# Windowed attention feeding a token and channel mixer: products with v per pair of heads, q and k parts a slot ahead

## Chip, cores and metric

The kernel runs on one core of a Trainium2 chip. The metric is the device time of one launch in microseconds (us). The engines named below are TensorE (PE, with PEld for its weight loads), VectorE (DVE), ScalarE (ACT), GpSimd (POOL) and SyncE (SP), which issues the DMAs.

## What is computed

Eight batches of eight heads, 576 positions, head width 64. Attention runs within a causal window of 128 with a bias that falls with distance; its output is the input of a mixer with a cosine and sine turn, a token mix and a channel mix.

```python
def _attn_ref(q, k, v):
    scores = scale * np.matmul(q, k.transpose(0, 1, 3, 2))
    ...
    mask = (rel >= 0) & (rel < window)
    scores = np.where(mask, scores + bias[None], -1000000000.0)
    scores = scores - np.max(scores, axis=-1, keepdims=True)
    attn = np.exp(scores)
    attn = attn / (np.sum(attn, axis=-1, keepdims=True) + 1e-09)
    return np.matmul(attn, v)

def _moe_ref(x, w_theta, w_tok_r, w_tok_i, w_ch):
    theta = x @ w_theta
    zr, zi = x * np.cos(theta), x * np.sin(theta)
    y = np.einsum('ts,bsd->btd', w_tok_r, zr) + np.einsum('ts,bsd->btd', w_tok_i, zi)
    u = x + y
    return u + np.maximum(u @ w_ch, 0.0)
```

## The kernel before

**Tiling.** Two heads make a pair, four pairs a batch. A pair's scores fall into five tiles: tile 0 goes to a bank of the pool `ps_m`, tiles 1 and 2, and 3 and 4, to two-bank buffers of `ps_s`. PSUM has eight banks here: two buffers of `ps_s` (4), one bank of `ps_a` (`acc`), three of `ps_m`. Operands are split into a high and a low part, so that one product is three matmuls: `qh`, `kh`, `ql`, `kl` in `split_pair` (ACT L336 and L339, DVE L337, POOL L340), `vh`, `vl` in `split_values` (ACT L361, POOL L362, DVE L363).

**A pair's way.** `weigh` (DVE L428) adds the bias and takes the row's limit, ACT L431 takes the exponential into `front` (tiles 0 to 2) and `back` (tiles 3 and 4). `flip` makes two fp16 parts of each half (`hl`, ACT L445 and DVE L447), and a DMA on SP turns them (L449) into `pt`. A slot later `Head.values` (L467) makes the products of `pt` with `vh` and `vl`, 27 matmuls a head, in `acc`, and `Head.finish` (L480) clears it into `x_sb` with three DVE instructions: L484 (the sums), L486 (reciprocal), L487 (the scaled copy of 128 x 320). `acc` has one buffer, so the second head's products wait for the first head's L487.

**Stages.** `start` does the attention of batch 0 and unpacks the weights (up to 73 us). Then follow, for each batch b, a `turn` (transposes of `x_sb`, theta, sine and cosine, parts `z_hi` and `z_lo`) and four slots of `attend(b + 1)`. A slot holds the scores of the next pair, the products with v of the present one, and steps of two generators for batch b: `mix` (token mix, three matmuls a step) and `channels`. TensorE's order is the order of the code (L72 pins it): `STEPS` says how many steps stand at the slot's front, behind the scores (two entries, in a row) and behind the first head's products. The last pair of numbers of a slot thus cover the first head's `finish` and the second head's. Slots 1 and 3 also end a group of four heads: `measure` (DVE L260) has taken the largest |v|, `spread_first` and `spread_scales` make a scale from it, with a small matmul `mm<-fixed` that waits for DVE L272.

**Order on DVE, ACT, SP.** The other engines' order comes from a scheduler with priorities (`high_priority`) and `issue_after`. `prepare(p + 3)`, behind the first head's `finish`, makes the q and k parts for the pair of the next slot and then issues the loads of the following pair into `qr` and `kr`, which have one buffer each. `kl` on POOL waits for `ql` by hand (L342).

## Times and profile before

| | us |
|---|---|
| median of three runs | 697.14 (696.0 to 699.99) |
| the profiled execution, its own time | 699.51 |
| its span in the trace | 697.7 |
| busy: PE, DVE, ACT, POOL | 632.0, 543.5, 502.1, 147.2 |
| mean granted TensorE clock | 0.978 of full speed |

Busy time is read per engine over the span. A row of waits names the engine, the buffer and line that waited, the engine and line waited for, and then the sum in us, the number of waits and the longest. A row of a timeline has start, duration, engine, line, operation and, in brackets, the idle time just before and what ended it.

### The profile page before, as it was taken

What the parts mean: (1) busy time and instruction counts of PE and PEld (TensorE: products, weight loads), DVE (VectorE), ACT (ScalarE), POOL (GpSimd) and SP (SyncE); (2) the same over time, 40 slices, a digit from 0 to 9 for tenths busy, and PEclk for the clock granted to TensorE, in tenths of its full rate; (3) what the DMA queues carried; (4) which work ended last, traced back from release to release, by engine and by line L of the source; (5) the groups of instructions that cost most, each with busy time, mean ns of one, the idle gap of its engine ahead of it and who ended that gap; (6) DMA issues with size and microseconds to landing.
All of it is one profiled execution on the core that took longest, in us unless ns stands there. A gap on an engine that the chain in (4) does not pass through costs nothing.

```text
span 697.7 us, 15147 instructions
## 1 busy us (share of the span) xinstructions
PE 632.0 (91%) x5738; PEld 537.4 (77%) x5738; DVE 543.5 (78%) x1463; ACT 502.1 (72%) x947; POOL 147.2 (21%) x198
## 2 busy tenths in 40 slices
PE   4899697689999999799989999799989999799998
PEld 3888475468877888688867888688867888689887
DVE  4989679788699868898689868898689968865722
ACT  6999379666986769766977769766977679745810
POOL 3010000433113112131212212131212212220220
PEclk9999999799999999999999999999999999999999
DMA  9954702769128840788036940677047930731001
GB/s 273 322 169 134 129 0 58 188 120 199 37 53 193 163 116 18 145 157 190 25 79 159 185 95 18 157 156 187 18 82 155 157 85 18 150 76 36 27 18 52
DMA packets 153257, 80.22 MB, mean 115 GB/s; under 512 B 126304, under 2 KB 142688, under 8 KB 153184
## 3 DMA queue, kind: packets, MB, share of 16 engines
q1 hardware_dynamic: 153184, 79.25, 49.7%
q8 instruction: 45, 0.74, 0.4%
q14 instruction: 28, 0.23, 0.1%
HBM read 39.39 MB, written 9.44 MB: 70 GB/s over the span
## 4 chain that ended last, share of the span: by engine, by line
ACT 38%; DVE 28%; PE 21%; issue 7%; DMA 4%; POOL 1%; SPq 0%; DVEq 0%; ACTq 0%; POOLq 0%
PE mm L75 16%; ACT hl L445 6%; ACT back L431 6%; ACT front L431 5%; DVE hl L447 5%; ACT g L552 3%; ACT z_hi L500 2%; ACT g L551 2%; DVE vl L363 2%; PE acc L75 2%; DVE ql L337 2%; DVE x_sb L487 2%; DVE front L428 2%; DVE g L556 2%; ACT xtf L525 2%
## 5 line engine op out<-in xcount | busy, mean ns | idle before, releaser
L75 PE MATMUL mm<-wtk_hi,z_hi 128*128 128x288 f16 x576 | 168.7, 293 | 0.4 <-DVE f L548 0.4
L75 PE MATMUL mm<-wtk_lo,z_hi 128*128 128x288 f16 x576 | 168.3, 292 | 0.0
L75 PE MATMUL mm<-wtk_hi,z_lo 128*128 128x288 f16 x576 | 168.1, 292 | 0.1
L75 PEld LDWEIGHTS <-z_hi 128*128 128x128 f16 x1152 | 109.5, 101 | 31.8 <-issue 1.3
L431 ACT ACTIVATE front<-front,fixed 128x256 f32<-128x256 f32 (+2 forms) x160 | 61.1, 448 | 45.8 <-DVE fixed L428 45.8
L75 PE MATMUL acc<-vh,pt 128*128 128x65 f16 x1044 | 60.5, 198 | 28.6 <-DVE x_sb L487 25.4
L75 PEld LDWEIGHTS <-pt 128*128 128x128 f16 x1566 | 56.4, 101 | 36.3 <-DVE x_sb L487 22.3
L340 POOL TENSOR_TENSOR kl<-kr,kh 128x576 fp32r<-128x576 f32 x31 | 48.5, 1564 | 136.6 <-DVE ql L337 40.1
L75 PEld LDWEIGHTS <-z_lo 128*128 128x128 f16 x576 | 57.6, 100 | 16.3 <-DVE z_lo L501 0.6
L622 POOL TENSOR_TENSOR u_lo<-xtf,u_hi 128x288 fp32r<-128x288 f32 x64 | 52.3, 837 | 58.1 <-ACT u_hi L620 31.0
L75 PE MATMUL acc<-vl,pt 128*128 128x64 f16 x522 | 56.7, 197 | 0.0
L361 ACT ACTIVATE vh<-vb,fixed 128x320 f16<-128x320 f32 x58 | 32.4, 562 | 33.7 <-PE acc L75 29.7
L431 ACT ACTIVATE back<-back,fixed 128x256 f32<-128x256 f32 x128 | 56.6, 498 | 0.0
L620 ACT CAST u_hi<-xtf 128x288 fp32r<-128x288 f32 x64 | 27.1, 426 | 37.5 <-DVE xtf L618 36.8
L362 POOL MEMSET vh<- 128x5 f16 x58 | 6.9, 119 | 220.6 <-PE acc L75 180.0
L75 PE MATMUL mm<-wth_hi,x_hi 128*128 128x512 f32 x160 | 48.0, 423 | 0.7 <-DVE x_hi L518 0.7
L75 PE MATMUL mm<-u_hi,wch_hi 128*128 128x288 f32 x256 | 47.2, 306 | 0.0
L428 DVE CUSTOM_DVE_ANT_0 back<-ps,bands 128x256 f32<-128x256 f32 x128 | 46.5, 419 | 0.1
L618 DVE SCALAR_TENSOR_TENSOR xtf<-mm,fixed,xtf 128x288 f32<-128x288 f32 x64 | 32.3, 508 | 18.1 <-PE mm L75 17.9
L75 PE MATMUL mm<-wth_lo,x_hi 128*128 128x512 f32 x160 | 44.8, 402 | 0.0
L75 PE MATMUL ps<-kh,qh 64*128 64x256 f32 (+1 forms) x256 | 43.8, 341 | 0.8 <-DVE fixed L428 0.8
L75 PE MATMUL mm<-u_lo,wch_hi 128*128 128x288 f32 x256 | 44.4, 295 | 0.0
(161 smaller groups left out, 1585.4 us busy)
## 6 DMA issues: line engine op xcount, KB each, us to landing
vb<-in_vx_dram SPq DMA_DIRECT2D x16, 650.0 KB, 5.1
out_dram<-xtf SPq DMA_DIRECT2D x64, 144.0 KB, 1.8
kr<-in_kt_dram SPq DMA_DIRECT2D x31, 288.0 KB, 3.5
qr<-in_qt_dram SPq DMA_DIRECT2D x31, 144.0 KB, 3.4
qr<-in_qt_dram SPq DMA_DIRECT2D x31, 128.0 KB, 3.4
xtf<-in_wch_dram SPq DMA_DIRECT2D x4, 512.0 KB, 4.8
z_hi<-in_wtok_dram SPq DMA_DIRECT2D x2, 576.0 KB, 6.3
z_lo<-in_wtok_dram SPq DMA_DIRECT2D x2, 576.0 KB, 6.3
```

The source lines that it names most:

```text
L75: ins = nc.tensor.matmul(*args, **kw)
L337: low = nc.vector.scalar_tensor_tensor(out=ql, in0=qr, scalar=sc, in1=qh.bitcast(F32), op0=ALU.mult, op1=ALU.subtract)
L340: rest = nc.gpsimd.tensor_tensor(out=kl, in0=kr, in1=kh.bitcast(F32), op=ALU.subtract)
L361: nc.scalar.activation(vh[:, :, :64], v, AF.Copy, scale=vs)
L428: self.weighed = nc.vector.tensor_tensor_reduce(out=sb, in0=ps, in1=bias, scale=2.0 ** -(2 * self.p % H + 1), scalar=3.0e38, op0=ALU.add, ...
L431: self.exps.append(nc.scalar.activation(sb, sb, AF.Exp, bias=least, scale=-1.0))
L445: self.copied = nc.scalar.activation(hl[:, 0], src, AF.Copy, scale=2.0 ** PEXP)
L447: self.lowered = nc.vector.scalar_tensor_tensor(out=hl[:, 1], in0=src, scalar=2.0 ** PEXP, in1=hl[:, 0], op0=ALU.mult, op1=ALU.subtract)
L552: nc.scalar.activation(g[:n], g[:n], AF.Sin, bias=halfpi[:n], scale=-RAD)
L618: nc.vector.scalar_tensor_tensor(out=xtf[:, m, cs], in0=y_ps[:, :HALF], scalar=st["back"], in1=xtf[:, m, cs], op0=ALU.mult, op1=ALU.add)
L620: nc.scalar.copy(u_hi[:, m, cs], xtf[:, m, cs])
L622: return nc.gpsimd.tensor_tensor(out=u_lo[:, m, cs], in0=xtf[:, m, cs], in1=u_hi[:, m, cs].bitcast(F32), op=ALU.subtract)
```

## The change

A pair's `values` now makes both heads' products, 54 matmuls in a row, in one two-bank buffer of `ps_s`; `ps_a` is gone and `ps_m` has four banks. `Pair.finish` clears both heads with three DVE instructions of twice the size. What stood between the two heads' products (the fourth entry of `STEPS`, `spread_scales`, a step of `channels`) now stands behind both. `split_pair` is cut into `split_high` (the two ACT instructions), called at the slot's front before the scores, and `split_low` (`ql`, `kl`), called with `prepare`'s loads behind the slot's last `weigh`; the parts made are those of the pair two slots on, one more than before. `vh` and `vl` have four buffers for two.

```diff
@@ -35,7 +35,7 @@
-RINGS = ([("mx", 2 * NT, 4)] + [("den", NT, 6)] + [("whole", 1, 3), ("vs", GROUP, 3), ("scale", GROUP, 4)]
+RINGS = ([("mx", 2 * NT, 4)] + [("den", 2 * NT, 3)] + [("whole", 1, 3), ("vs", GROUP, 3), ("scale", GROUP, 4)]
@@ -55,7 +55,7 @@
-    vp = ctx.enter_context(tc.tile_pool(name="vp", bufs=2))
+    vp = ctx.enter_context(tc.tile_pool(name="vp", bufs=4))
@@ -66,8 +66,7 @@
-    ps_a = ctx.enter_context(tc.tile_pool(name="ps_a", bufs=1, space=PSUM))
-    ps_m = ctx.enter_context(tc.tile_pool(name="ps_m", bufs=3, space=PSUM))
+    ps_m = ctx.enter_context(tc.tile_pool(name="ps_m", bufs=4, space=PSUM))
@@ -328,15 +327,23 @@
         batch_scale(0, scale[:, :8])
 
     def split_pair(p, raw):
+        return split_low(split_high(p, raw))
+
+    def split_high(p, raw):
 
         qr, kr = raw
         qh, ql = (qk.tile([128, S + 64], F32R, name=name) for name in ("qh", "ql"))
         kh, kl = (qk.tile([128, S], F32R, name=name) for name in ("kh", "kl"))
         sc = -0.125 * 2.0 ** (2 * p % H + 1)
         nc.scalar.activation(qh, qr, AF.Copy, scale=sc)
+        nc.scalar.copy(kh, kr)
+        return qr, kr, qh, ql, kh, kl, sc
+
+    def split_low(made):
+
+        qr, kr, qh, ql, kh, kl, sc = made
         low = nc.vector.scalar_tensor_tensor(out=ql, in0=qr, scalar=sc, in1=qh.bitcast(F32), op0=ALU.mult,
                                              op1=ALU.subtract)
-        nc.scalar.copy(kh, kr)
         rest = nc.gpsimd.tensor_tensor(out=kl, in0=kr, in1=kh.bitcast(F32), op=ALU.subtract)
         if pinned:
             after(rest, low)
@@ -351,10 +358,11 @@
             vb = group_v[n // GROUP]
             if n < 2 * PLAIN:
                 return (vb[:, k],), None, None
-            vs = first_scale[0][:, n:n + 1]
+            both = first_scale[0][:, n - n % 2:n - n % 2 + 2]
         else:
             vb, scale = group_v[n // GROUP]
-            vs = scale[:, k:k + 1]
+            both = scale[:, k - k % 2:k - k % 2 + 2]
+        vs = both[:, n % 2:n % 2 + 1]
         v = vb[:, k, :, :64]
         vh = vp.tile([128, 5, 65], F16, name="vh")
         vl = vp.tile([128, 5, 64], F16, name="vl")
...
@@ -454,38 +462,45 @@
                     at = 128 * n + (64 * to if i == 0 else 0)
                     self.pt[i, to, j] = [t[:, at:at + 128] for t in parts_of]
 
+        def values(self):
+            acc = ps_s.tile([128, 2, 512], F32, name="ps")
+            self.acc = acc[:, :, :NT * 65].rearrange("p e (i d) -> p e i d", d=65)
+            for head in self.heads:
+                e = head.h % 2
+                for i in (0, 2, 3, 4, 1) if e == 0 else (0, 1, 2, 3, 4):
+                    prods = []
+                    for j, c in enumerate(CHUNKS[i]):
+                        for a, part in enumerate(self.pt[i, e, j]):
+                            for o, v in enumerate(head.v):
+                                if a + o < len(head.v):
+                                    prods.append((part, v[:, c, :65 if o == 0 else 64]))
+                    for n, (l, r) in enumerate(prods):
+                        mm(self.acc[:, e, i, :r.shape[-1]], l, r, start=(n == 0), stop=(n == len(prods) - 1))
+
+        def finish(self, x_sb):
+            h = self.heads[0].h
+            den = rings["den"].take().rearrange("p (e i) -> p e i", e=2)
+            tiny = 1.0e-9 * (1.0 if self.early else 2.0 ** PEXP)
+            vs = self.heads[0].vs
+            if vs is None:
+                nc.vector.tensor_scalar(out=den, in0=self.acc[:, :, :, 64], scalar1=tiny, scalar2=None, op0=ALU.add)
+            else:
+                nc.vector.scalar_tensor_tensor(out=den, in0=self.acc[:, :, :, 64], scalar=tiny,
+                                               in1=vs[:, :, None].broadcast_to([128, 2, NT]), op0=ALU.add,
+                                               op1=ALU.mult)
+            nc.vector.reciprocal(out=den, in_=den)
+            x = x_sb[:, :, h * D:(h + 2) * D].rearrange("p i (e d) -> p e i d", e=2)
+            return nc.vector.tensor_tensor(out=x, in0=self.acc[:, :, :, :64],
+                                           in1=den[:, :, :, None].broadcast_to([128, 2, NT, D]), op=ALU.mult)
+
     class Head:
         def __init__(self, n, pair):
             self.n, self.pair = n, pair
             self.b, self.h = divmod(n, H)
-            self.tiny = 1.0e-9 * (1.0 if pair.early else 2.0 ** PEXP)
 
         def ready(self):
             self.v, self.vs, low = split_values(self.n)
             return low
-
-        def values(self):
-            self.acc = ps_a.tile([128, 512], F32, name="acc")
-            av = self.acc[:, :NT * 65].rearrange("p (i d) -> p i d", d=65)
-            for i in (0, 2, 3, 4, 1) if self.h % 2 == 0 else (0, 1, 2, 3, 4):
-                prods = []
-                for j, c in enumerate(CHUNKS[i]):
-                    for a, part in enumerate(self.pair.pt[i, self.h % 2, j]):
-                        for e, v in enumerate(self.v):
-                            if a + e < len(self.v):
-                                prods.append((part, v[:, c, :65 if e == 0 else 64]))
-                for n, (l, r) in enumerate(prods):
-                    mm(av[:, i, :r.shape[-1]], l, r, start=(n == 0), stop=(n == len(prods) - 1))
-
-        def finish(self, x_sb):
-            av = self.acc[:, :NT * 65].rearrange("p (i d) -> p i d", d=65)
-            den = rings["den"].take()[:, :, None]
-            scaled = {} if self.vs is None else {"op1": ALU.mult}
-            nc.vector.tensor_scalar(out=den, in0=av[:, :, 64:65], scalar1=self.tiny, scalar2=self.vs,
-                                    op0=ALU.add, **scaled)
-            nc.vector.reciprocal(out=den, in_=den)
-            return nc.vector.tensor_tensor(out=x_sb[:, :, self.h * D:(self.h + 1) * D], in0=av[:, :, :64],
-                                           in1=den.broadcast_to([128, NT, D]), op=ALU.mult)
 
 
     def turn(x_sb, st):
@@ -692,8 +706,14 @@
 
             steps = STEPS[min(g, 2)] if b > 1 else FIRST[g]
             step(mixing, steps[0])
+            ahead = p + DEPTH + 1
+            made = split_high(ahead, raw.pop(ahead)) if ahead < pairs else None
             for tiles in SCORES:
                 scores(tiles)
+            if made is not None:
+                with tc.issue_after(new.weighed.ins):
+                    parts[ahead] = split_low(made)
+                    prepare(ahead + 1)
             if new is not None:
                 new.flip(0)
                 new.flip(1)
@@ -706,9 +726,10 @@
             if scaled:
                 with tc.high_priority(FINISH):
                     spread_first(scaled)
-            one.values()
+            pair.values()
             with tc.high_priority(FINISH):
-                done = one.finish(x_sb)
+                done = pair.finish(x_sb)
+            step(mixing, steps[3])
             if scaled:
                 with tc.high_priority(FINISH):
                     spread_scales(scaled)
@@ -718,17 +739,11 @@
                         measure(*some)
                 if new is not None:
                     new.heads[0].ready()
-                with tc.issue_after(new.copied.ins) if new is not None else nullcontext():
-                    prepare(p + DEPTH + 2)
                 if b == 1 and g == 0:
                     with behind_all(new.exps):
                         step(late)
-            step(mixing, steps[3])
             if g >= 2 and (b > 1 or g == 3):
                 step(chans)
-            two.values()
-            with tc.high_priority(FINISH):
-                done = two.finish(x_sb)
             if new is not None:
                 with tc.issue_after(done.ins):
                     done = new.heads[1].ready()
@@ -768,18 +783,14 @@
                 pace(2 * len(tiles))
 
             if last is not None:
-                one, two = last.heads
                 last.flip(0)
                 scores(SCORES[0])
                 scores(SCORES[1])
                 last.flip(1)
-                one.values()
+                scores(SCORES[2])
+                last.values()
                 with tc.high_priority(FINISH):
-                    one.finish(x_sb)
-                scores(SCORES[2])
-                two.values()
-                with tc.high_priority(FINISH):
-                    two.finish(x_sb)
+                    last.finish(x_sb)
             else:
                 for tiles in SCORES:
                     scores(tiles)
```

The order of the built programs shows three places. First TensorE in slot 0 of a batch (matmuls and their weight loads), where the first head's products had ended and mixing matmuls lay ahead of the second head's. Before:

```order
2372 L75 MATMUL mm<-wtk_lo,z_hi 128x288
2373 L75 LDWEIGHTS z_lo
2374 L75 MATMUL mm<-wtk_hi,z_lo 128x288
2375 L75 LDWEIGHTS pt
2376 L75 MATMUL acc<-vh,pt 128x65
```

After, the seam between the two heads in the same slot (the first head's last product is row 2347):

```order
2345 L74 MATMUL ps<-vl,pt 128x64
2346 L74 LDWEIGHTS pt
2347 L74 MATMUL ps<-vh,pt 128x65
2348 L74 LDWEIGHTS pt
2349 L74 MATMUL ps<-vh,pt 128x65
```

The second head's products follow the first's at once, in another bank; the nine mixing matmuls that lay between now lie behind row 2401, ahead of the next slot's scores.

Second, DVE in slot 0 of the same batch, from the slot's `measure` to the first products of the next slot (`fixed` holds the small rings, `den` among them; `xtf` is the token mix's sum). Before:

```order
613 L260 TENSOR_REDUCE peak_107<-vb 128x2
614 L447 SCALAR_TENSOR_TENSOR hl<-front_105,hl 128x1024
615 L618 SCALAR_TENSOR_TENSOR xtf<-mm,fixed,xtf 128x288
616 L295 TENSOR_SCALAR peak_107<-peak_107 128x4
617 L618 SCALAR_TENSOR_TENSOR xtf<-mm,fixed,xtf 128x288
618 L447 SCALAR_TENSOR_TENSOR hl<-back,hl 128x1024
619 L484 TENSOR_SCALAR fixed<-acc,fixed 128x5
620 L486 RECIPROCAL fixed<-fixed 128x5
621 L487 TENSOR_TENSOR x_sb<-acc,fixed 128x5x64
622 L337 SCALAR_TENSOR_TENSOR ql<-qr,qh 128x640
623 L363 SCALAR_TENSOR_TENSOR vl<-vb,fixed,vh 128x320
624 L484 TENSOR_SCALAR fixed<-acc,fixed 128x5
```

After:

```order
571 L345 SCALAR_TENSOR_TENSOR ql<-qr,qh 128x640
572 L259 TENSOR_REDUCE peak_104<-vb 128x2
573 L455 SCALAR_TENSOR_TENSOR hl<-front_102,hl 128x1024
574 L633 SCALAR_TENSOR_TENSOR xtf<-mm,fixed,xtf 128x288 x2
575 L294 TENSOR_SCALAR peak_104<-peak_104 128x4
576 L455 SCALAR_TENSOR_TENSOR hl<-back,hl 128x1024
577 L488 SCALAR_TENSOR_TENSOR fixed<-ps,fixed 128x10
578 L491 RECIPROCAL fixed<-fixed 128x10
579 L493 TENSOR_TENSOR x_sb<-ps,fixed 128x2x5x64
580 L371 SCALAR_TENSOR_TENSOR vl<-vb,fixed,vh 128x320 x2
```

`ql`, and with it POOL's `kl`, has moved from behind the first clearing to ahead of both `hl` instructions; three clearing instructions stand where six did, in the place of the first head's.

Third, SP's queue in slot 0. Before, the slot's two turning DMAs, then the loads of q and k:

```order
100 L449 DMA_TRANSPOSE pt<-hl 128x16x128 x2
101 L238 DMA qr<-in_qt_dram 64x576
102 L239 DMA qr<-in_qt_dram 64x512
103 L240 DMA qr<-in_qt_dram 64x64
104 L241 DMA kr<-in_kt_dram 128x576
```

After:

```order
103 L237 DMA qr<-in_qt_dram 64x576
104 L238 DMA qr<-in_qt_dram 64x512
105 L239 DMA qr<-in_qt_dram 64x64
106 L240 DMA kr<-in_kt_dram 128x576
107 L457 DMA_TRANSPOSE pt<-hl 128x16x128 x2
```

The loads, which wait for the slot's `ql` and `kl` to have read `qr` and `kr`, now stand ahead of the turning DMAs.

## Rows read from the trace of the kernel before

**Rows 1.** The page's busy row, and its row of waits for `acc`.

```profile
PE 632.0 (91%) x5738; PEld 537.4 (77%) x5738; DVE 543.5 (78%) x1463; ACT 502.1 (72%) x947; POOL 147.2 (21%) x198
...
PE acc L75 <- DVE x_sb L487: 25.6, 16, 3.3
```

**Rows 2.** TensorE's waits from 190 to 612 us, six batches' slots.

```profile
PE acc L75 <- DVE x_sb L487: 20.1, 12, 3.3
PE ps L90 <- DVE x_sb L487: 2.3, 5, 0.5
PE mm L75 <- DVE fixed L272: 2.1, 5, 0.4
```

**Rows 3.** Timeline of slot 0 of one batch: DVE, then TensorE.

```profile
282.62 1.23 DVE L447 SCALAR_TENSOR_TENSOR hl<-back,hl 128x1024 f16<-128x1024 f32 x1 [0.54 <-ACT hl L445]
283.77 0.22 DVE L484 TENSOR_SCALAR fixed<-acc,fixed 128x5 f32<-128x5 f32 x1
284.02 0.19 DVE L486 RECIPROCAL fixed<-fixed 128x5 f32<-128x5 f32 x1
284.24 0.49 DVE L487 TENSOR_TENSOR x_sb<-acc,fixed 128x320 f32<-128x320 f32 x1
...
284.79 0.23 PE L75 MATMUL acc<-vh,pt 128*128 128x65 f16 x1 [3.29 <-DVE x_sb L487]
```

**Rows 4.** Windows of that batch's four slots (stretch, length, busy by engine, clock).

```profile
272.60:288.00 15.40, 12.11 (x141) 9.83 (x139) 13.57 (x39) 12.40 (x23) 1.77 (x3) 0.89 0.52 73
288.00:299.80 11.80, 11.01 (x139) 9.03 (x137) 10.66 (x37) 8.43 (x17) 3.35 (x5) 1.00 0.80 185
299.80:312.40 12.60, 12.31 (x150) 10.47 (x152) 11.80 (x41) 8.33 (x17) 3.73 (x8) 1.00 0.80 137
312.40:324.70 12.30, 11.89 (x143) 10.33 (x141) 11.23 (x35) 8.53 (x18) 2.87 (x5) 1.00 1.00 208
```

**Rows 5.** Windows of slot 0 of the four later batches.

```profile
350.20:365.80 15.60, 12.29 (x142) 9.89 (x139) 13.71 (x39) 12.53 (x23) 1.95 (x4) 0.90 0.40 81
428.20:443.40 15.20, 11.89 (x142) 9.49 (x140) 13.90 (x39) 12.54 (x23) 1.77 (x3) 0.93 0.40 79
506.20:520.90 14.70, 11.40 (x141) 9.19 (x140) 13.52 (x39) 12.54 (x23) 1.68 (x3) 0.96 0.38 75
584.20:598.40 14.20, 10.88 (x142) 9.01 (x139) 13.01 (x38) 12.53 (x23) 1.20 (x2) 1.00 0.35 70
```

**Rows 6.** Timeline of TensorE from a second head's products to the next scores.

```profile
596.52 0.20 PE L75 MATMUL acc<-vh,pt 128*128 128x65 f16 x1 [3.32 <-DVE x_sb L487]
...
600.06 0.28 PE L75 MATMUL ps<-kh,qh 64*128 64x256 f32 x2
```

**Rows 7.** POOL's `kl` beside DVE's `vl`, and two DVE groups (count | sum, mean ns).

```profile
322.03 1.44 POOL L340 TENSOR_TENSOR kl<-kr,kh 128x576 fp32r<-128x576 f32 x1 [3.50 <-DVE ql L337]
322.18 1.63 DVE L363 SCALAR_TENSOR_TENSOR vl<-vb,fixed,vh 128x320 f16<-128x320 f32 x1
...
L363 DVE SCALAR_TENSOR_TENSOR vl<-vb,fixed,vh 128x320 f16<-128x320 f32 x58 | 37.9, 657 | 0.5 <-ACT vh L361 0.5
L260 DVE TENSOR_REDUCE peak<-vb 128x2 f32<-128x640 f32 x26 | 21.1, 813 | 0.0
```

**Rows 8.** SP's queue and TensorE: turning DMAs of slot 0, products of slot 1.

```profile
281.23 4.70 SPq L449 DMA_TRANSPOSE pt<-hl  x2
...
pt<-hl SPq DMA_TRANSPOSE x58, 4.6
...
293.86 0.19 PE L75 MATMUL acc<-vh,pt 128*128 128x65 f16 x1
```

**Rows 9.** Batch 1's slots: one window, and TensorE's waits there.

```profile
103.50:174.00 70.50, 56.99 (x588) 45.96 (x589) 60.66 (x167) 49.29 (x97) 20.43 (x24) 0.88 0.64 138
...
PE mm L75 <- POOL kl L340: 3.9, 2, 2.5
PE acc L75 <- DVE x_sb L487: 3.3, 2, 2.7
```

More of the change, by code (lines that the diff above doesn't have):

```diff
@@ L364, in split_values @@
                                              op1=ALU.subtract)
-        return (vh, vl), vs, low
+        return (vh, vl), both, low
     TILES = [(512, 64, 384, 192, 0), (0, 128, 0, 128, 128), (128, 128, 0, 256, 0), (256, 128, 128, 256, 0),
@@ L673, in attend @@
             pair = first.pop(0)
-            one, two = pair.heads
             new = None
```

## The prediction

> **What bounds the kernel now.** I read the page's busy row first: TensorE is busy 632.0 us of the span [rows 1], so what it stands idle, some 66 us, is about all that a change of order can give, apart from time lost to a lower clock. The waits say where a good part of it goes: 25.6 us in 16 waits are for `acc`, the one bank that the second head's products find uncleared [rows 1]; 20.1 us in 12 of them lie between 190 and 612 us [rows 2]. The timeline shows one: TensorE has been idle 3.29 us when the second head's products start at 284.79, right behind the end of `x_sb` (284.24 + 0.49), and that clearing stood behind the `hl` of the back half, which had itself waited 0.54 us for ScalarE [rows 3]. So in slot 0 the nine mixing matmuls between the heads don't cover the clearing, which comes late on VectorE. The windows tell how much room there is behind it. Slot 0 takes 15.40 us with TensorE busy 12.11 at a granted clock of 0.89, VectorE 13.57; the other three slots run at clock 1.00 with TensorE busy 11.01, 12.31 and 11.89 of 11.80, 12.60 and 12.30 us, and VectorE 10.66, 11.80 and 11.23 [rows 4]. VectorE is thus never far behind TensorE, and in slot 0 it is ahead of it. That is what limits the change.
>
> **The waits for `acc`.** With both heads in two banks, the second head's products need no clearing, and the 20.1 us go. What takes their place is one ring further: a pair's two-bank buffer is the one that the next slot's scores of tiles 3 and 4 are written to, so they wait for `x_sb`. In slot 0, TensorE stood ready at 284.79 - 3.29 = 281.50. From the second head's first product to those scores is 600.06 - 596.52 = 3.54 us [rows 6], the same work in another order, so it now comes to them at 285.0. The clearing ended at 284.73; it comes later by the larger size and by what `kl` costs (both below: 0.3 and up to 0.7), so at up to 285.75. I take a new wait of 0.75 us in each of six slots 1, 4.5 us in all; from below it is zero, if the 0.54 us of rows 3 take up the delay. Net 15.6.
>
> **The clearing.** A head's three instructions take 0.22, 0.19 and 0.49 us, 0.90 in all [rows 3]. The first two work on 5 columns, so some 0.2 of each is fixed; by that the copy of 640 columns takes 0.2 + 2 x 0.29 = 0.78 and a pair 1.19 us instead of 1.80. Bounds: 0.90 (nothing per column) and 1.80. VectorE gets back 0.6 us a slot, or between 0.9 and 0; I count 0.5, 2.0 a batch.
>
> **Small waits.** Five waits of the turn's first transposes for `x_sb` (2.3 us) go, since the last clearing now has mixing and channel steps behind it. The five waits for L272 (2.1 us) [rows 2] don't go: the small matmul still stands in slot 1, and VectorE comes out of slot 0 later than TensorE by the 0.75 us above; I take 1.0 us each, 5.0 in all. Together a loss of 0.6.
>
> **The clock.** In the windows of slot 0 the granted clock is 0.89, 0.90, 0.93, 0.96 and 1.00 [rows 4, 5], while every other slot there has 1.00. At full clock they would lose 0.11 x 15.40 + 0.10 x 15.6 + 0.07 x 15.2 + 0.04 x 14.7 = 5.0 us less. The last of them kept 1.00 with a wait of 3.32 us [rows 6], so a wait doesn't always lower it. I take 4.0, from 0 to 5.0.
>
> **`ql` and `kl` moved.** They cost the same instructions, but next to other work. Before, `kl` ran beside `vl`: `vl` took 1.63 us, having started 0.15 us behind a `kl` of 1.44, while its mean over 58 is 657 ns [rows 7]. So VectorE stood for about 1 us there, once a batch. In the new order `kl` starts at the end of `ql`, and the next instruction with two operands in SBUF is the `hl` of the front half. In slot 0 only the peak of 0.81 us [rows 7] lies between; VectorE stands for 1.44 - 0.81 = 0.6 to 0.7 us. In the other slots a token mix sum lies between as well, and I take half, 0.3. That is 1.6 a batch against 1.0 given back. Bounds: nothing, and all of `kl`, 1.44 in each slot.
>
> The Trainium skill's page "SBUF — State Buffer", section "Who interferes with whom", states that a VectorE instruction with two SBUF inputs contends with a GpSimd instruction that reads SBUF, that the one which starts first keeps the shared ports, and that reductions don't contend. The trace agrees on the first (1.63 against 657 ns). It speaks against this place of `kl`; by it alone the whole rest of `kl` behind the peak, 0.6 us, falls on `hl` in slot 0, which is what the sum has.
>
> **Loads on SP.** The four loads go ahead of the slot's turning DMAs and wait for `ql` and `kl`, which now come before `hl` on VectorE; so nothing that isn't late already holds them. The turning DMAs were issued from 281.23, 4.70 us for both, landing 4.6 us behind their issue, and the products that need them start at 293.86 [rows 8]: even 3 us later they land in time. The loads themselves get a whole slot until the next slot's `qh`. I count nothing; if the cover were gone, each us would be one us of slot.
>
> **Batch 1.** There the waits are 3.9 us for `kl` and 3.3 for `acc`, and the clock is 0.88 over 70.50 us [rows 9], a loss of 8.5. The q and k parts are now a slot ahead, so both waits go (7.2); half of the clock comes back (4.2). Against it, the back half's `hl` in slot 0 now stands behind the first `weigh` of slot 1, so `pt` comes late, at most by its landing of 4.6 us [rows 8]. 7.2 + 4.2 - 4.6 = 6.8; VectorE is busy 60.66 of the 70.50 already, so it can't give more than 9.8 + 2 anyway. I take 6, from 2 to 11.
>
> **Start.** 25.6 - 20.1 - 3.3 = 2.2 us of waits for `acc` lie ahead of batch 1. They go, but the second head's products no longer run beside the first head's clearing. I take 1, from -2 to 4.
>
> **The sum.** 15.6 - 0.6 + 4.0 + 6 + 1 = 26.0 us. The profiled execution took 699.51, so 673.5; the median of the runs stands at 697.14 / 699.51 = 0.9966 of it, so 671.2, about 671 us.
>
> **Rival 1: VectorE becomes the bound of all slots.** Over the four slots it is busy 13.57 + 10.66 + 11.80 + 11.23 = 47.26 of 52.10 us [rows 4]. The change takes 2.0 and 1.0 from it and adds 1.6, so 45.9; TensorE needs 10.88 (slot 0 at full clock [rows 5]) + 11.01 + 12.31 + 11.89 = 46.1. They are level. If VectorE keeps the 4.84 us that it stands idle now (for ScalarE's `hl`, for matmuls), the slots take 50.7, a gain of 1.4 a batch, 8.4 in six, with 7 for batch 1 and the start 15.4: 684.1, as a median 681.8. For it: in slot 0 VectorE is busier than TensorE in every batch. Against it: its idle time is partly that caused by TensorE's waits, and slots 2 and 3 let it catch up.
>
> **Rival 2: nothing takes the waits' place.** The 20.1, 2.3 and 2.1 us, the clock's 5.0, 8.5 in batch 1 and 2 at the start are 40.4: 659.1, as a median 657. Against it: it leaves VectorE almost no idle time in slots 0 and 1.
>
> **Rival 3, slower: `kl` stops VectorE in every slot.** If the `hl` behind it stands for the whole 1.44 us in each slot and the idle 4.84 us stay, the slots take 47.26 - 3.0 + 5.76 + 4.84 = 54.9, 2.8 more than now; six batches lose 16.6, batch 1 and the start give 3: 713, as a median 711. It decides from 52.10 - 4.84 - 44.26 = 3.0 us a batch, 0.75 a slot. For it, `kl` did that to `vl` [rows 7]; against it, the peak and the token mix sum stand between.
>
> **How the numbers follow.** Forecast 671: 0.60 (662 to 679, the ends by the clock, batch 1 and the new waits). Rival 1, 682: 0.21 (676 to 691). Rival 2, 657: 0.08. Rival 3, 711: 0.06. The rest, 0.05, is that gains and new waits cancel, within half a per cent, which is about what a measurement here can tell from no change (3.5 us). Range 660 to 687: beyond it lie rival 3, most of the cancelling case, much of rival 2 and a little of rival 1, together 0.2. Faster by over 0.5%: 0.87; the same 0.06; slower 0.07.
>
> **What would show it.** The row of waits for `acc` must be gone, and a row of scores in `ps` waiting for `x_sb` must stand at some 0.75 us in slots 1; 0.5 there or 2 would move the sum by 1.5 or 7 us. Slot 0 should take some 12 us at a clock near 1.00. A pair's copy should take 0.78 us. `hl` of the front half should show durations above 1.23 us where `kl` runs, by 0.3 to 0.7. Batch 1's window should be some 64 us. The forecast is wrong if VectorE's busy share in the slots goes above 0.95, or if TensorE waits for `pt` or `qh`.

## The result and the profile after

| | before | after |
|---|---|---|
| median, us | 696.89 (696.0 to 699.99, 4 runs) | 667.89 (667.4 to 668.83, 4 runs) |
| the profiled execution, us | 699.51 | 667.59 |
| span in the trace, us | 697.7 | 665.8 |
| busy PE / DVE / ACT, us | 632.0 / 543.5 / 502.1 | 609.4 / 525.7 / 500.0 |

The ratio of the medians is 0.9578, with a 95% interval from 0.9546 to 0.961: the change is faster by 29 us. The prediction was 671, within 660 to 687.

The mean granted clock of the whole run fell, from 0.978 to 0.954: the first 73 us ran at 0.71 here and at 1.00 before. The time doesn't show it: what lies ahead of batch 1 took 1.5 us less all the same, and executions of the kernel before with means from 0.931 to 0.983 took 696 to 700 us.

Where the waits for `acc` stood [rows 2], the same stretch of the changed kernel (TensorE's waits from 190 to 605 us) has:

```profile
PE mm L74 <- DVE fixed L271: 5.8, 10, 0.9
PE ps L74 <- DVE x_sb L493: 4.3, 5, 0.9
PE mm L74 <- DVE x_hi L533: 1.4, 2, 0.9
```

The 20.1 us for `acc` are gone. In their place stand five waits of scores for `x_sb`, at most 0.9 us, and ten for the small matrix of L271, two a batch (five, 2.1 us, before [rows 2]). The turn's transposes don't wait for `x_sb` any more; two of its x parts wait instead.

The timeline of slot 0 shows how that wait comes about (POOL, DVE, then TensorE; it answers to [rows 3]):

```profile
270.66 1.42 POOL L347 TENSOR_TENSOR kl<-kr,kh 128x576 fp32r<-128x576 f32 x1 [9.61 <-issue]
...
271.17 1.99 DVE L455 SCALAR_TENSOR_TENSOR hl<-front,hl 128x1024 f16<-128x1024 f32 x1
...
274.01 1.21 DVE L455 SCALAR_TENSOR_TENSOR hl<-back,hl 128x1024 f16<-128x1024 f32 x1
275.14 0.16 DVE L488 SCALAR_TENSOR_TENSOR fixed<-ps,fixed 128x10 f32<-128x10 f32 x1
275.33 0.22 DVE L491 RECIPROCAL fixed<-fixed 128x10 f32<-128x10 f32 x1
275.58 0.82 DVE L493 TENSOR_TENSOR x_sb<-ps,fixed 128x640 f32<-128x640 f32 x1
...
276.55 0.39 PE L74 MATMUL ps<-kh,qh 64*128 64x256 f32 x2 [0.86 <-DVE x_sb L493]
```

`hl` of the front half takes 1.99 us where its mean was 1219 ns before:

```profile
L447 DVE SCALAR_TENSOR_TENSOR hl<-front,hl 128x1024 f16<-128x1024 f32 x29 | 35.3, 1219 | 4.5 <-ACT hl L445 4.4
```

It starts beside `kl` and takes 0.77 us more. The pair's clearing is 0.16, 0.22 and 0.82 us. The scores of tiles 3 and 4 of the next slot start 0.15 us behind its end.

The windows of the same batch's four slots and of the turn behind them answer to [rows 4] (length, then busy PE, PEld, DVE, ACT and POOL with counts, clock, DMA share, GB/s):

```profile
263.60:274.20 10.60, 10.60 (x140) 8.99 (x138) 10.60 (x31) 9.99 (x18) 1.48 (x2) 1.00 0.14 41
274.20:286.70 12.50, 10.93 (x139) 8.91 (x136) 12.33 (x37) 7.49 (x15) 3.27 (x6) 1.00 1.06 221
286.70:297.80 11.10, 11.10 (x143) 9.66 (x142) 9.81 (x35) 9.21 (x20) 3.03 (x4) 1.00 0.56 117
297.80:309.60 11.80, 10.94 (x140) 9.49 (x138) 11.45 (x35) 7.33 (x16) 3.23 (x6) 1.00 1.08 239
309.60:337.60 28.00, 27.46 (x171) 24.12 (x169) 17.80 (x30) 24.46 (x44) 6.14 (x6) 1.00 0.28 67
```

The clock is 1.00 throughout. VectorE is busy 10.60 of 10.60 us in slot 0 and 12.33 of 12.50 in slot 1; in slots 0 and 2 TensorE has no idle time, in slots 1 and 3 it waits. (A part of the mixing has moved from the slots into the turn, so slots can't be compared one by one, batches can.)

The whole of batches 2 to 7, from the first score matmul to the end, before and then after:

```profile
197.36:697.70 500.34, 469.73 (x4572) 401.00 (x4569) 385.76 (x1044) 349.12 (x659) 110.41 (x148) 0.99 0.48 103
```

```profile
192.42:665.80 473.38, 458.21 (x4572) 396.19 (x4569) 372.49 (x972) 345.35 (x656) 106.22 (x146) 1.00 0.51 109
```

Of the 26.96 us given here, TensorE's idle time gives 30.61 - 15.17 = 15.4, and its busy time, with the same 4572 matmuls, gives 11.5 (taken apart in the section on the prediction). Batch 1 (first score to first score) went from 93.86 to 90.45 us, a gain of 3.4; what lies ahead of it gave 1.5.

### The profile page after: what moved, and what is told of

It is laid out like the page before. It is cut to its first block, busy times and chain, and to the rows that moved or that the text cites. A ratio compares the mean times of both kernels' runs of the same rounds, so it can differ in the third digit from the quotient of the medians.

```text
span 665.8 us, 15029 instructions
## 1 busy us (share of the span) xinstructions
PE 609.4 (92%) x5738; PEld 524.8 (79%) x5738; DVE 525.7 (79%) x1367; ACT 500.0 (75%) x947; POOL 143.2 (22%) x198
## 4 chain that ended last, share of the span: by engine, by line
DVE 30%; PE 29%; ACT 22%; DMA 12%; issue 4%; SPq 1%; POOL 0%; DVEq 0%; ACTq 0%; POOLq 0%
PE mm L74 23%; DMA qr<-in_qt_dram 8%; PE ps L74 5%; DVE hl L455 5%; DMA pt<-hl 4%; DVE front L436 3%; ACT g L567 3%; DVE back L436 2%; ACT g L566 2%; ACT z_hi L515 2%; DVE z_lo L516 2%; DVE g L571 2%; DVE vl L371 2%; ACT front L439 2%; DVE ql L345 2%
## 5 line engine op out<-in xcount | busy, mean ns | idle before, releaser
L74 PE MATMUL mm<-wtk_hi,z_hi 128*128 128x288 f16 x576 | 165.8, 288 | 0.6 <-ACT z_hi L515 0.6
L74 PE MATMUL mm<-wtk_hi,z_lo 128*128 128x288 f16 x576 | 165.1, 287 | 0.5 <-DVE z_lo L516 0.3
L74 PE MATMUL mm<-wtk_lo,z_hi 128*128 128x288 f16 x576 | 165.2, 287 | 0.0
L74 PEld LDWEIGHTS <-z_hi 128*128 128x128 f16 x1152 | 107.6, 99 | 30.7 <-ACT z_hi L515 0.9
L347 POOL TENSOR_TENSOR kl<-kr,kh 128x576 fp32r<-128x576 f32 x31 | 44.7, 1443 | 145.6 <-issue 72.7
L74 PE MATMUL ps<-vh,pt 128*128 128x65 f16 x1044 | 56.9, 199 | 12.4 <-DMA pt<-hl 12.2
L74 PE MATMUL ps<-vl,pt 128*128 128x64 f16 x522 | 54.6, 197 | 0.0
L338 ACT ACTIVATE qh<-qr 128x640 fp32r<-128x640 f32 x31 | 22.9, 739 | 41.4 <-DMA qr<-in_qt_dram 41.2
L455 DVE SCALAR_TENSOR_TENSOR hl<-front,hl 128x1024 f16<-128x1024 f32 x29 | 46.6, 1606 | 2.7 <-ACT hl L453 2.5
L74 PE MATMUL mm<-u_hi,wch_lo 128*128 128x288 f32 x256 | 44.6, 296 | 0.0
```

The costliest lines, as they stand in the source:

```text
L74: ins = nc.tensor.matmul(*args, **kw)
L338: nc.scalar.activation(qh, qr, AF.Copy, scale=sc)
L347: rest = nc.gpsimd.tensor_tensor(out=kl, in0=kr, in1=kh.bitcast(F32), op=ALU.subtract)
L455: self.lowered = nc.vector.scalar_tensor_tensor(out=hl[:, 1], in0=src, scalar=2.0 ** PEXP, in1=hl[:, 0], op0=ALU.mult, op1=ALU.subtract)
```

## Experiments

Each run stands beside runs of the kernel before on the same chip; its ratio to those is given with its interval.

**The products alone.** Pairs as in the changed kernel, the q and k parts in their old place.

```diff
-            ahead = p + DEPTH + 1
-            made = split_high(ahead, raw.pop(ahead)) if ahead < pairs else None
...
-            if made is not None:
-                with tc.issue_after(new.weighed.ins):
-                    parts[ahead] = split_low(made)
-                    prepare(ahead + 1)
...
                     new.heads[0].ready()
+                with tc.issue_after(new.copied.ins) if new is not None else nullcontext():
+                    prepare(p + DEPTH + 2)
```

> The changed kernel, but q and k parts made in the old place, behind the pair's clearing, for the next slot. Theory A (the gains of the two halves add up): the waits for acc are gone all the same, about 675 us. Theory B (the one half needs the other): the clearing of both heads now ends at about the time of the next slot's first score matmul or 2 us behind it, and ql (0.8) and kl (1.4) stand behind it, so TensorE waits 2.5 to 4.5 us for ql and kl in three slots of each batch, 9 us a batch net: 710 to 725 us, slower than the kernel before.

Measured: 715.67 us, ratio 1.0258 (1.0224 to 1.0291). TensorE's waits over the whole run:

```profile
PE mm L74 <- POOL kl L347: 20.5, 16, 2.8
PE mm L74 <- DVE ql L345: 16.2, 9, 2.8
```

Theory B. The waits for `acc` are gone, and longer ones for `kl` and `ql` have taken their place: a clearing that covers both heads ends too late for parts that queue behind it.

**The parts alone.** The kernel before, with the parts made at the slot's front.

```diff
...
             step(mixing, steps[0])
+            ahead = p + DEPTH + 1
+            made = split_high(ahead, raw.pop(ahead)) if ahead < pairs else None
             for tiles in SCORES:
                 scores(tiles)
+            if made is not None:
+                with tc.issue_after(new.weighed.ins):
+                    parts[ahead] = split_low(made)
+                    prepare(ahead + 1)
...
-                with tc.issue_after(new.copied.ins) if new is not None else nullcontext():
-                    prepare(p + DEPTH + 2)
```

> The kernel before, but q and k parts made at the slot's front, a slot ahead. Theory A: the short waits of the first score tile for kl go (about 5 us over all), 690 to 693 us. Theory B: ql (0.8) and the hl beside kl (0.3 to 0.8 longer) now stand ahead of the first head's clearing, so the wait for acc grows from 3.3 to 4.3 or 4.8 us in slot 0 and shows up with 0.5 to 1.5 us in other slots: 698 to 712 us.

Measured: 724.89 us, ratio 1.0391 (1.0362 to 1.042), beyond both expectations on the slow side. TensorE's waits from 190 to 640 us:

```profile
PE mm L75 <- DVE fixed L272: 25.6, 11, 2.6
PE acc L75 <- DVE x_sb L495: 22.2, 11, 3.5
```

Theory B in direction, but not by its number: the wait for `acc` grew little (22.2 in this stretch). What I had not priced is the small matmul of `spread_scales`. It stands between the heads here, behind 27 products only, and now waits up to 2.6 us for L272, which stands on VectorE behind the later `hl`. The change's other edit, which puts that matmul behind both heads and the mixing, takes this away: in the changed kernel L271 has at most 0.9. So each half of the change is slower than the kernel before, by 2.6 and 3.9%, and both together are faster by 4.2%. The four buffers for `vh` and `vl` were in the first run and not in the second; they weren't tested by themselves.

**`kl` cut short.** The changed kernel, with 64 of 576 columns of `kl` made; the rest stays zero.

```diff
...
-        rest = nc.gpsimd.tensor_tensor(out=kl, in0=kr, in1=kh.bitcast(F32), op=ALU.subtract)
+        rest = nc.gpsimd.tensor_tensor(out=kl[:, :64], in0=kr[:, :64], in1=kh[:, :64].bitcast(F32), op=ALU.subtract)
```

> The changed kernel, with kl made for 64 of its 576 columns only (the rest of it stays zero). Theory A (VectorE's stand beside kl is on the path in slots 0 and 1): hl of the front half falls from 1.61 to about 1.23 us on average, the scores' wait for x_sb from 0.86 to 0.2 and those for L271 by half, 660 to 663 us. Theory B (hidden): hl falls the same way and the time stays at 667 to 668 us.

Measured: 665.52 us, ratio 0.9547 (0.9513 to 0.958), against 0.9578 (0.9546 to 0.961) of the changed kernel: between the two expectations, and the intervals overlap. VectorE's group in the changed kernel and then in this one:

```profile
L455 DVE SCALAR_TENSOR_TENSOR hl<-front,hl 128x1024 f16<-128x1024 f32 x29 | 46.6, 1606 | 2.7 <-ACT hl L453 2.5
```

```profile
L459 DVE SCALAR_TENSOR_TENSOR hl<-front,hl 128x1024 f16<-128x1024 f32 x29 | 35.7, 1229 | 0.8 <-ACT hl L457 0.5
```

All of what this `hl` takes over its 1.22 us is `kl`: 10.9 us of VectorE's time. Only some 2 of them reach the end, and that isn't clear of the noise. The scores' waits for `x_sb` are 2.8 us in five here, where the changed kernel has 4.3.

**Two clearings.** The changed kernel, with three clearing instructions for each head.

```diff
...
-            nc.vector.reciprocal(out=den, in_=den)
-            x = x_sb[:, :, h * D:(h + 2) * D].rearrange("p i (e d) -> p e i d", e=2)
...
+            for e in range(2):
+                den = both[:, e, :, None]
...
+                nc.vector.reciprocal(out=den, in_=den)
+                done = nc.vector.tensor_tensor(out=x_sb[:, :, (h + e) * D:(h + e + 1) * D], in0=av[:, :, :64],
+                                               in1=den.broadcast_to([128, NT, D]), op=ALU.mult)
```

> The changed kernel, with the pair cleared by six instructions, three for each head, as in the kernel before. Theory A (VectorE is on the path in slots 0 and 1): a pair's clearing takes 1.8 instead of 1.2 us, the scores' wait for x_sb grows to 1.4, the waits for L271 and the turn's first transposes too, 671 to 675 us. Theory B: at most 1 us more, 668 to 669 us.

Measured: 674.94 us, ratio 0.9672 (0.964 to 0.9704), theory A. TensorE's waits from 190 to 610 us:

```profile
PE ps L74 <- DVE x_sb L492: 7.1, 5, 1.4
PE mm L74 <- DVE fixed L271: 5.3, 8, 1.0
```

The scores' wait is the expected 1.4 us. One clearing for both heads is thus worth some 7 us; 2.8 of them stand in the first row (4.3 in the changed kernel), and 3.1 lie ahead of batch 2, whose first score starts at 195.54 us against 192.42; the rest was not followed up.

**Short loads.** The changed kernel, with 64 columns or fewer of q and k loaded for later pairs.

```diff
...
+        if p > H // 2 + 1:
+            nc.sync.dma_start(out=q[:64, :64], in_=qt[b, h, :, :64])
+            nc.sync.dma_start(out=q[64:, :32], in_=qt[b, h + 1, :, :32])
+            nc.sync.dma_start(out=q[64:, S:S + 32], in_=qt[b, h + 1, :, 512:544])
+            nc.sync.dma_start(out=kr[:, :64], in_=kt[b, h:h + 2, :, :64].rearrange("h d s -> (h d) s"))
+            return q, kr
```

> The changed kernel, with the loads of q and k cut from 576 to 64 or fewer columns from the seventh pair on (older values stay in the rest). Theory A (the 41 us that ScalarE stands for qr are hidden behind TensorE's own work): those waits shrink to half or less and the time stays within 2 us of the changed kernel's, 666 to 669 us. Theory B (they hold up vh, and with it VectorE and the next slot): VectorE's wait for vh in slot 2 (1.2 us a batch) goes, and TensorE's waits for x_sb and L271 behind it, 657 to 662 us.

Measured: 663.98 us, ratio 0.9529 (0.9506 to 0.9552), between the two; the interval just overlaps that of the changed kernel. ScalarE's wait for `qr` fell from 41.2 us in 21 waits to 19.7 in 17. TensorE's rows from 190 to 605 us:

```profile
PE mm L74 <- DVE fixed L278: 5.1, 10, 0.9
PE ps L74 <- DVE x_sb L500: 4.3, 5, 0.9
```

The waits for `x_sb` are those of the changed kernel and the ones for L271 are 0.7 us shorter, so theory B's way, by VectorE to these two, is hardly there. But the changed kernel's two waits for `x_hi` (1.4 us) are gone. In the changed kernel they come from the load: the turn's `x_hi` stands on ScalarE behind `qh` (and `kh` and `vh`), and `qh` stands for `qr` (ScalarE, then TensorE):

```profile
309.88 0.74 ACT L338 ACTIVATE qh<-qr 128x640 fp32r<-128x640 f32 x1 [3.72 <-DMA qr<-in_qt_dram]
...
313.37 0.35 ACT L532 CAST x_hi<-ps 128x256 fp32r<-128x256 f32 x1
...
314.23 0.97 PE L74 MATMUL mm<-wth_hi,x_hi 128*128 128x512 f32 x3 [0.54 <-DVE x_hi L533]
```

In the profiled execution batches 2 to 7 took 470.05 us against 473.36, batch 1 91.26 against 90.45, and what lies ahead of it 103.26 against 101.97, though the three waits for `pt` (two in batch 1, one ahead of it) fell from 12.2 to 8.2 us. So the gain stands behind batch 1, 3.3 us there. Lighter DMA traffic could give a part of it too; how much of it is ScalarE's wait stays open.

**Batch 1's unpacking later.** The changed kernel with the last weights' unpacking behind `hl`.

```diff
-                    with behind_all(new.exps):
+                    with tc.issue_after(new.lowered.ins):
                         step(late)
...
```

> The changed kernel, with the unpacking of the channel weights in batch 1 put behind VectorE's hl of the back half, where it was behind the slot's exponentials. Theory A (in batch 1 pt lands late because ScalarE's and VectorE's hl stand behind that unpacking): TensorE's three waits for pt (12.2 us) fall to 4 to 8, 661 to 665 us. Theory B (batch 1 is bound by VectorE's work, wherever it stands): other waits take their place, 666 to 670 us.

Measured: 669.64 us, ratio 0.9609 (0.9589 to 0.9629), theory B. TensorE's waits from 100 to 197 us:

```profile
PE ps L74 <- DVE x_sb L493: 3.3, 1, 3.3
PE mm L74 <- DVE fixed L271: 2.8, 1, 2.8
PE mm L89 <- DVE peak L294: 2.3, 1, 2.3
PE ps L74 <- DMA pt<-hl: 2.2, 1, 2.2
```

`pt` came in time but for 2.2 us of 9.4, and three waits for VectorE's results have 8.4 us where the changed kernel has 3.2. Batch 1 itself took 88.16 us against 90.45, and what lies ahead of it 105.25 against 101.97; with three banks (below), where only a bank is left idle, that took 104.93 too. So this place gives nothing in sum. That VectorE's work bounds batch 1 wherever it stands isn't shown: with `kl` beside the weighs (below) batch 1 took 86.87 us.

**Three banks.** The changed kernel with one PSUM bank left idle.

```diff
-    ps_m = ctx.enter_context(tc.tile_pool(name="ps_m", bufs=4, space=PSUM))
+    ps_m = ctx.enter_context(tc.tile_pool(name="ps_m", bufs=3, space=PSUM))
```

> The changed kernel, with three banks in the pool of the mixing sums, as before, and one PSUM bank left idle. Theory A (the fourth bank has no part in the gain): 667 to 670 us. Theory B (the sums wait for a bank once spread_scales' and the scores' banks stand among them behind a late VectorE): TensorE shows waits for a bank of mm of 0.5 us or more in each slot, 675 to 690 us.

Measured: 667.48 us, ratio 0.9571 (0.9549 to 0.9594): theory A. The fourth bank has no part in the gain.

**`kl` beside the weighs.** The changed kernel, with `kl` behind the slot's first `weigh`.

```diff
...
             for tiles in SCORES:
                 scores(tiles)
+                if tiles == (0,) and made is not None:
+                    _, kr, _, _, kh, kl, _ = made
+                    rest = nc.gpsimd.tensor_tensor(out=kl, in0=kr, in1=kh.bitcast(F32), op=ALU.subtract)
+                    after(rest, new.weighed)
```

> The changed kernel, with kl made behind the slot's first weigh, beside the weighs (one operand in PSUM), instead of behind ql. Theory A (kl stops only VectorE instructions with two operands in SBUF, and the place was what cost): hl of the front half falls from 1.61 to about 1.23 us, the weighs keep 0.42, 664 to 666 us, as with kl cut short. Theory B (kl slows whatever VectorE does): the weighs grow by about as much as hl falls, 667 to 669 us.

Measured: 692.71 us, ratio 0.9934 (0.9909 to 0.9958): neither. `hl` of the front half fell to 1216 ns and the long weighs kept 417, as theory A has it, and yet nearly all of the gain was gone. The timeline of slot 1 shows why (ScalarE, VectorE, TensorE):

```profile
289.36 0.67 ACT L339 CAST kh<-kr 128x576 fp32r<-128x576 f32 x1 [2.69 <-DMA kr<-in_kt_dram]
289.94 1.05 ACT L452 ACTIVATE hl<-back 128x1024 f16<-128x1024 f32 x1
...
291.02 1.22 DVE L454 SCALAR_TENSOR_TENSOR hl<-back,hl 128x1024 f16<-128x1024 f32 x1 [2.35 <-ACT hl L452]
292.16 0.22 DVE L271 TENSOR_SCALAR fixed<-fixed 128x4 f32<-128x4 f32 x1
...
292.44 0.38 PE L74 MATMUL mm<-fixed 128*128 128x4 f32 x2 [3.27 <-DVE fixed L271]
```

With `kl` earlier, the scheduler also put ScalarE's `kh` of the next pair ahead of `hl` of the back half. There it stands 2.69 us for its load, `hl` behind it, VectorE behind that, and TensorE 3.27 us at the end. In three of the five slots 1 TensorE's wait for L271 is over 3 us; in the other two it is 0.9 and 0.3. The next run holds ScalarE's order.

**The same, with ScalarE's order held.** `qh` and `kh` behind the slot's `hl`, and `kl` behind the first `weigh` of tile 1.

```diff
...
-            made = split_high(ahead, raw.pop(ahead)) if ahead < pairs else None
+            with tc.issue_after(pair.copied.ins):
+                made = split_high(ahead, raw.pop(ahead)) if ahead < pairs else None
             for tiles in SCORES:
                 scores(tiles)
+                if tiles == (1, 2) and made is not None:
...
+                    after(rest, new.begun)
```

> The changed kernel, with kl beside the weighs again, now behind the first weigh of tile 1, and qh and kh held behind ScalarE's hl of the back half. Theory A (in the run before, only the place of kh cost: ScalarE stood 2.7 us for the load of kr with hl of the back half behind it): the 3.3 us waits for L271 go back under 1 us, hl of the front half stays at 1.22 us, 662 to 666 us. Theory B (kl beside the weighs costs by itself, as beside z_lo and g in slot 0): 670 us or more.

Measured: 664.87 us, ratio 0.9528 (0.9503 to 0.9552), theory A; the interval overlaps that of the changed kernel. The row for L271 over the whole run, 15.0 us in the run before, is back to:

```profile
PE mm L74 <- DVE fixed L271: 4.6, 6, 0.8
```

The two runs differ in `kl`'s start too, by one `weigh`: in the first, `kl` met the instruction of L570 in slot 0 (1.90 us, where the same one takes 0.75 in the changed kernel) and `vl` in slot 2 (1.71 for 0.54), and both stood for more than a microsecond. So the 27.8 us between them are ScalarE's order and that place together, and were not taken apart; the chain above shows that the first has a part in it in slot 1.

**Mixing moved ahead of the waiting scores.** The changed kernel, with two steps of mixing at the front of slot 1.

```diff
-STEPS, FINISH = ((7, 7, 6, 3), (3, 4, 6, 4), (3, 4, 6, 3)), 250
+STEPS, FINISH = ((7, 7, 6, 3), (5, 2, 6, 4), (3, 4, 6, 3)), 250
```

> The changed kernel, with two steps of the token mix (6 matmuls, 0.73 us) moved in slot 1 from behind the scores to the slot's front. Theory A (the scores' wait for x_sb is a gap in TensorE's work alone): it falls from 0.86 to 0.2 us or less and six batches give 3 to 5 us, 663 to 665 us. Theory B (VectorE is the bound of slots 0 and 1): the wait moves to L271 in the same slot, which grows from 0.7 to about 1.3, and the time stays at 667 to 669 us.

Measured: 669.85 us, ratio 0.9595 (0.9566 to 0.9624), theory B, a little above its range. From 190 to 605 us:

```profile
PE mm L74 <- DVE fixed L271: 8.0, 10, 1.7
PE ps L74 <- DMA pt<-hl: 2.3, 5, 0.7
```

The scores no longer wait there, and L271 took the wait over, from 5.8 to 8.0 us. This fits a VectorE that bounds slots 0 and 1 of the changed kernel (busy 10.60 of 10.60 and 12.33 of 12.50 us): to cover its lateness in one place only moves it to the next.

**Both.**

> Both of the two edits before together. Theory A: VectorE is relieved by kl's new place, so both waits fall and the gains add, 658 to 663 us. Theory B: 662 to 668 us.

Measured: 661.66 us, ratio 0.9494 (0.9467 to 0.9521), theory A, near the border of the two expectations, and the fastest kernel that computes everything. From 190 to 605 us it waits only here:

```profile
PE mm L74 <- DVE fixed L271: 4.8, 5, 1.3
PE ps L74 <- DMA pt<-hl: 0.7, 3, 0.3
```

The shift of mixing that gave nothing by itself goes with the fastest time once VectorE has its time back from `kl`. Its interval lies clear below that of the changed kernel (0.9546 to 0.961), by some 6 us. It overlaps that of `kl` alone with ScalarE's order held (0.9503 to 0.9552), so what the mixing adds there isn't shown.

## Why the prediction was right, and where it was off

The profiled execution gave 31.9 us, and the sum had 26.0. The medians gave 29.0; the profiled execution of the kernel before was 2.4 us above its median. That the sum and the medians are so close is in part luck: TensorE's busy time in batches 2 to 7 gave 7.5 us more than was put, and batch 1 2.6 less. By the sum's steps:

- **The waits for `acc`: right.** 20.1 us went, and the new wait of scores for `x_sb` is 0.8 to 0.9 us in five of the six slots 1 where 0.75 in each was put: 4.3 against 4.5. The cause was as told, `kl` beside `hl` and the larger clearing ahead of it.
- **The clearing: right.** 0.82 us for the copy against 0.78, and 0.16 and 0.22 for the rest. Two clearings cost 7 us, for which the sum had no term of its own.
- **Small waits: right in size, split otherwise.** L271 has 5.8 us in ten waits, two a batch, where 5.0 in five was put; two waits of the turn for `x_hi`, 1.4, were not foreseen (see the loads below).
- **The clock: right in kind, too small.** It is 1.00 in the slots after. The sum read it from slot 0 alone [rows 4, 5], but in three of the four batches the lower clock runs on into slot 1. The four stretches in the kernel before:

```profile
284.30:287.70 3.40, 2.91 (x34) 2.36 (x35) 2.78 (x7) 1.16 (x3) 1.65 (x2) 0.50 1.09 167
362.80:366.20 3.40, 3.40 (x35) 2.69 (x32) 2.23 (x6) 0.56 (x1) 2.23 (x3) 0.50 0.99 198
441.30:444.70 3.40, 3.40 (x24) 2.52 (x22) 2.22 (x7) 0.56 (x1) 2.92 (x4) 0.50 1.00 213
519.80:523.20 3.40, 3.40 (x22) 2.79 (x22) 1.78 (x5) 0.79 (x2) 2.74 (x4) 0.50 1.22 155
```

  TensorE is busy 13.1 us in them at half clock, so they cost up to 6.6 us (an estimate: half of that time), where 4.0 was put.
- **`ql` and `kl` beside `hl`: right.** `hl` took some 1.99 us in five of the six slots 0 and 1.56 in slots 1 to 3 (2.28 behind the last `kl`, with no peak ahead of it), against 1.22 before: 0.77 and 0.34 more, where 0.6 to 0.7 and 0.3 were put. The Trainium skill's page "SBUF — State Buffer", section "Who interferes with whom", has a VectorE instruction with two SBUF inputs contend with a GpSimd instruction that reads SBUF. The trace agrees both ways: `hl` is longer beside `kl`, and `vl`, whose mean was 657 ns when some of them ran beside `kl` [rows 7], has 546 away from it.
- **The step that was mis-sized: what TensorE's busy time holds.** The sum counted rows of idle time and the clock, 19.0 us for batches 2 to 7; 26.96 came. Idle time gave 15.4, close to the 15.0 that was put (15.6 - 0.6). Busy time gave 11.5 where only the clock's 4.0 was put. Besides the clock, the rest stood in the first score tile, where TensorE waited for `kl` in pieces of 0.3 us. The view by tile gives lowest, median and highest ns of its third matmul, before and then after:

```profile
L75 PE MATMUL mm<-kl,qh x23: 269/355/416, 197.7 to 610.7; 128*128 128x192 f32 x23
```

```profile
L74 PE MATMUL mm<-kl,qh x23: 273/274/277, 192.7 to 579.1; 128*128 128x192 f32 x23
```

  And the timeline of one slot's second and third matmul, before (with POOL's `kl`) and then after:

```profile
309.97 1.60 POOL L340 TENSOR_TENSOR kl<-kr,kh 128x576 fp32r<-128x576 f32 x1 [3.28 <-DVE ql L337]
...
311.25 0.27 PE L75 MATMUL mm<-kh,ql 128*128 128x192 f32 x1
311.62 0.36 PE L75 MATMUL mm<-kl,qh 128*128 128x192 f32 x1
```

```profile
286.85 0.27 PE L74 MATMUL mm<-kh,ql 128*128 128x192 f32 x1
286.96 0.27 PE L74 MATMUL mm<-kl,qh 128*128 128x192 f32 x1
```

  0.37 us from start to start against 0.11, with no idle time shown, and the third matmul starts 0.05 us behind the end of `kl`. It does so in 13 of the 23 slots. Taken from start to start, the 69 matmuls of tile 0 in these batches and what follows each take 17.4 us before and 11.5 after; 1.0 of the 5.9 lies in the three slots 1 whose first scores ran at half clock, so the wait for `kl` is 4.9 us. With the clock's 6.6 at most, that covers the 11.5. The run with the parts alone, which makes `kl` a slot ahead in the kernel before, shows the cause: there no third matmul starts at the end of a `kl`, and the median is 277:

```profile
L75 PE MATMUL mm<-kl,qh x23: 272/277/416, 195.3 to 634.4; 128*128 128x192 f32 x23
```

  The prediction saw `kl` in batches 2 to 7 as a cost of the change only, and no term had this wait. TensorE's rows of waits hardly have it, but those of its weight loads do (190 to 612 us, before), under the name of POOL's next instruction, which these matmuls don't read:

```profile
PEld mm L75 <- POOL vh L362: 3.9, 13, 0.3
```

- **Batch 1: too high.** 3.4 us instead of 6. The clock rose from 0.91 to 0.94 over the batch, which gives back 3.0 where 4.2 was put, and the wait for `pt` behind the late `hl`, put once at 4.6, came twice, 4.65 and 4.74. What bounds batch 1 beyond these waits stays open.
- **Loads on SP: nothing was counted, and there was a cost.** ScalarE now stands 41.2 us for `qr`. "A whole slot" was too generous a cover: the loads are issued behind `ql`, with the turning DMAs behind them. TensorE's two waits for `x_hi` follow from it, 1.4 us; with the loads cut short they are gone, and batches 2 to 7 took 3.3 us less. In the run with `kh` ahead of `hl` such a wait ended in TensorE's 3.27 us.
- **The rivals.** Rival 1 (VectorE the bound of all slots, 682) was half right: the run with mixing moved fits it for slots 0 and 1, but not for 2, where TensorE has no idle time. What it had wrong is the 4.84 us of VectorE's idle time that were to stay: 1.81 are left in the four slots (busy 44.19 of 46.00). Rival 2's terms add up to 40.0, not 40.4, which moves its median by 0.4 us; the last experiment comes near its 657, but by further edits. Rival 3's point, 0.75 us of standing a slot, was reached in slot 0 and behind the last `kl` only.
- **The signs of being wrong.** Two that the prediction named came out, although the time was right: VectorE's busy share in the four slots is 0.96, above 0.95, and TensorE waits 12.2 us for `pt`, 9.4 of them in batch 1. (The one wait for `qh`, 8.7 us, is that of the start, 8.4 before.)
- **What the prediction didn't see at all** is that its terms don't stand apart. It priced two halves and added them. Each half alone loses 18 to 27 us, since each removes a wait that the other alone makes.

## What to carry to other kernels

Before adding up the gains of two edits, ask what each would do alone: if one makes results later and the other makes their readers wait for something earlier, the pair has one gain, not two. Where TensorE waits in small pieces, its rows of idle time hardly show it; read those of its weight loads, and compare the shortest and the median duration, and start to start, of the first matmuls that read a fresh operand. When an instruction is moved on one engine, look at what the scheduler does on the others: an early load can put its reader at the head of an in-order queue.

## What the runs showed that was not expected

- With `kh` ahead of `hl`, ScalarE's queue turned 2.69 us of waiting for a load into 3.27 us of TensorE's time in the slot 1 shown (over 3 us in three of five), by way of `hl` on ScalarE and on VectorE, with no wait of TensorE's that names the load.
- `kl` on GpSimd stops VectorE's `hl` (1219 to 1606 ns on average) but not its weighs, which read one operand from PSUM (the long ones average 419 ns with `kl` beside `hl`, and 417 with `kl` beside the weighs, where each that ran beside it took 0.42 us).
- The last of the slots 0 kept the clock at 1.00 before, over a wait of 3.32 us [rows 5, 6], while it fell to 0.50 at the end of each of the four others, also of 3.3 us, or up to 1.3 us behind it (the 0.89 to 0.96 of slot 0 differ by how much of the lower stretch lies in slot 1); nothing here settles why it fell at those and not at this one.
